# Items of an expert layer: nested branches, the first items' loads, and the order of gathers and stores, all reworked at once

## The chip, the cores and the metric

The kernel runs on one core of a Trainium2 chip. The metric is device time in microseconds of one execution, the median of the runs shown; lower is better. Engines are called TensorE (PE in rows, PEld its weight loads), VectorE (DVE), ScalarE (ACT), GpSimd (POOL) and SyncE (SP, which issues most DMAs).

## What is computed

Three layers follow one another, in float32.

```python
# 1: attention in chunks of 64 positions; 8 batches, 8 heads, 576 positions, head size 64
scores = q_c @ k_c.T / 8; attn = softmax(scores); out = attn @ v_c      # -> x [4608, 512]
# 2: dense layer
h = x @ w_in                       # [4608, 2048]
g = s * relu(h)**2 + b
x = g @ w_out                      # [4608, 512]
# 3: experts; one of 8 for each token, or none
do_compute = x @ w_skip > 0
e_idx = argmax(xc @ w_gate); gate_w = softmax(...)[e_idx]
y[mask] = gate_w * (relu(xc[mask] @ w1[e]) @ w2[e])   # w1 [8,512,1024], w2 [8,1024,512]
out = x; out[do_compute] = xc + y
```

## The kernel before

Every product that must be exact to float32 is made of three: a matrix is split into a high part (a copy by ScalarE into the product format, "split_hi") and a low part (what is left, a subtraction on VectorE, "split_lo"), and low x high, high x low and high x high are added in PSUM.

The 4608 tokens are 36 tiles of 128, in 13 chunks of 2 or 3 tiles (`SIZES`). For each chunk the dense layer runs 16 steps over the 2048 columns: `p1_mm` (a product group of 12), `p1_sq` (ScalarE: relu and square), `p1_g` (scale, bias and split), and two steps later `p2` (a product group into the accumulators). In chunks 0 and 1 the scale and bias are on ScalarE, in the others on VectorE. After a chunk, `evac` stores the plain result to `out`, the logits and the routing (`route_a` to `route_ids`) choose an expert for each token, the rows with their gate value are stored to a table in memory (`x1s`, by `route_row`, 528 values a row), and the token numbers are scattered into lists by expert (`idl`).

All this, and the first two expert items, is ordered by a planner (`Plan.run`): operations have an engine, a cost, what they must follow, and an urgency; the planner simulates the engines and writes instructions in the order that it finds. Each engine then runs its instructions strictly in this order. The planner's names used here: `a12_f`, `q12_f`, `g12_f`, `b12_f` are the four parts of step f of the last chunk (chunk 12), `rw` the stores of x1s rows, `s_n`, `s_1`, `s_2` the count of tokens by expert after eleven chunks and the choice of the two largest experts from it, `s_i`, `s_g` the loads of their lists and the gathers of their tokens, and `s_w00`, `s_w01`, `s_w10`, `s_w11` the loads of the raw weights of these two items (first digit the item, second 0 for `w1`, 1 for `w2`, 2 MB each). The raw weights go where the dense layer's second matrix was: item 0's into the buffers of `w_out` 0 to 7, which `b12_7` reads last, item 1's into 8 to 15, which `b12_15` reads last.

An expert item is one expert and up to 256 of its tokens (full item) or up to 128 (half item). Item 0 and item 1 are the two speculative ones. What is left is counted after the last chunk (`t_n` to `t_c`), and lists of full and half items are made (`tu`, `tb`); their number is only known on the chip, so the code holds 24 full items and 8 half items (twice, for an odd or even number of full items), each behind a branch on the counts `ca` and `ch`. In this data there are 11 full and 4 half items. All engines take each branch for themselves.

A full item (`full_item`) does eight groups `mm1` (12 products each, 256 columns), each followed by a relu and a split of the result, then transposes of the next item's tokens (`x_all`), then eight groups `mm2` (6 products each, 512 columns) into two accumulators. Beside them the next item's weights are split in 16 parts (`split`, u = 0 to 15). At the end `put_add` multiplies by the gate and adds the input row on VectorE, and `put_out` scatters the result to `out` by an indirect DMA on GpSimd. At the start of an item the tokens and weights of the item after next are loaded (`load_x`: a list by SyncE, then two gathers by GpSimd; `load_w`: two loads by SyncE). A half item (`half_item`) is built alike with other shapes: 24 products, 12 transposes, 24 products; four of its 16 splits have their low part on GpSimd (`split_part`). Half items nest: behind a branch that another follows, the item that loads more, in the Else the last one (`final`).

## Time and profile before

| | us |
|---|---|
| median of 3 runs | 1332.43 (1331.69 to 1333.62) |
| the profiled execution, its own time | 1333.88 |
| its span, first to last instruction | 1332.0 |
| TensorE busy | 1289.6 (97%) |
| TensorE weight loads busy | 1152.3 (87%) |
| VectorE busy | 959.4 (72%) |
| ScalarE busy | 582.8 (44%) |
| GpSimd busy | 165.7 (12%) |

Times in rows are us from the start of the span. Busy time is an average over the stages: attention and the dense layer run to about 935, the two speculative items to about 998, the full items to 1256, the half items to the end. The profile names for each instruction what ended the idle time before it. "issue" there means that the engine waited for nothing that the profile shows. TensorE's granted clock is 1.00 at 2.4 GHz and 0.50 at 1.2 GHz; a stretch's value is the mean.

### The profile page before, as it was taken

The page shows a single profiled execution, that of the slowest core. Times are in us where ns is not written, and L with a number is a line of the kernel's source. Part 1 is how long each engine was busy: PE and PEld are TensorE (multiplying, and loading weights), DVE is VectorE, ACT ScalarE, POOL GpSimd, SP SyncE. Part 2 cuts the span into 40 slices and gives each one's busy share as a digit, 9 for nine tenths or more (in the row PEclk, how much of TensorE's full clock was granted, in tenths as well). Part 3 has the DMA queues.
Part 4 walks back from the last instruction along what each step waited for, and adds up shares of the span by engine and source line. Part 5 has one row for each costly group of instructions (what it writes and reads, how often), then busy time and mean ns, then how long its engine had stood idle before and what let it go on. Part 6 is the DMA issues. An engine that isn't in the chain of part 4 may idle for free. (4 is left out here: it accounts for less than half of the span.)

```text
span 1332.0 us, 23920 instructions
## 1 busy us (share of the span) xinstructions
PE 1289.6 (97%) x9112; PEld 1152.3 (87%) x9115; DVE 959.4 (72%) x2341; ACT 582.8 (44%) x1206; POOL 165.7 (12%) x186
## 2 busy tenths in 40 slices
PE   7999999999999999999999999999899999999895
PEld 5888898999998999999999999999788999998773
DVE  6995587659495766859485766757688878787684
ACT  7887533232232333233232333232546656555472
POOL 0000001000101010100101010101122121121252
PEclk9999999999999999999999999999799999999998
DMA  7562324111214142131314131112969565666472
GB/s 270 186 198 104 66 79 88 40 48 48 49 48 73 48 44 77 33 64 49 49 48 73 48 50 56 17 33 81 260 220 391 190 232 221 221 255 220 162 288 90
DMA packets 43019, 160.46 MB, mean 120 GB/s; under 512 B 11370, under 2 KB 11754, under 8 KB 38142
## 3 DMA queue, kind: packets, MB, share of 16 engines
q1 hardware_dynamic: 36526, 142.55, 35.6%
q0 software_dynamic: 6352, 16.12, 3.5%
q8 instruction: 78, 1.28, 0.4%
q14 instruction: 63, 0.52, 0.1%
HBM read 132.68 MB, written 27.20 MB: 120 GB/s over the span
## 5 line engine op out<-in xcount | busy, mean ns | idle before, releaser
L332 ACT ACTIVATE r<-ph 128x384 f32<-128x384 f32 (+1 forms) x208 | 97.0, 466 | 418.0 <-PE ph L325 405.9
L325 PE MATMUL ph<-xh,win_l 128*128 128x384 f32 (+1 forms) x832 | 273.1, 328 | 0.0
L325 PE MATMUL ph<-xh,win_h 128*128 128x384 f32 (+1 forms) x832 | 270.1, 325 | 0.0
L325 PE MATMUL ph<-xl,win_h 128*128 128x384 f32 (+1 forms) x832 | 269.1, 323 | 0.0
L368 PE MATMUL acc<-wout_h,gl 128*128 128x512 f32 x544 | 218.7, 402 | 2.6 <-DVE gl L352 2.4
L349 DVE TENSOR_SCALAR r<-r,sb_sb 128x384 f32<-128x384 f32 (+1 forms) x176 | 84.3, 479 | 180.3 <-ACT r L333 180.0
L368 PE MATMUL acc<-wout_l,gh 128*128 128x512 f32 x544 | 214.1, 394 | 0.0
L368 PE MATMUL acc<-wout_h,gh 128*128 128x512 f32 x544 | 212.6, 391 | 0.0
L388 DVE CUSTOM_DVE_ANT_0 junk<-x,wl_sb 128x512 bf16<-128x512 f32 x270 | 185.7, 688 | 5.7
L325 PEld LDWEIGHTS ph<-xh,win_l 128*128 128x128 f32 x832 | 156.6, 188 | 7.0
L325 PEld LDWEIGHTS ph<-xl,win_h 128*128 128x128 f32 x832 | 156.7, 188 | 6.3
L325 PEld LDWEIGHTS ph<-xh,win_h 128*128 128x128 f32 x832 | 156.5, 188 | 0.0
L714 PE MATMUL ac<-win_h,hhl 128*128 128x512 f32 x480 | 155.1, 396 | 1.1 <-DVE hhl L795 1.0
L352 DVE TENSOR_TENSOR gl<-r,gh 128x384 fp32r<-128x384 f32 (+1 forms) x208 | 109.7, 527 | 31.4 <-ACT gh L339 25.1
L696 PE MATMUL ph<-xh,win_l 128*128 128x256 f32 x416 | 119.5, 287 | 5.7 <-ACT r L702 4.5
L368 PEld LDWEIGHTS acc<-wout_h,gh 128*128 128x128 f32 x544 | 102.1, 188 | 23.1
L368 PEld LDWEIGHTS acc<-wout_h,gl 128*128 128x128 f32 x544 | 102.1, 188 | 21.8 <-DVE gl L352 4.5
L696 PE MATMUL ph<-xl,win_h 128*128 128x256 f32 x416 | 119.0, 286 | 0.4 <-DVE xl L674 0.4
L658 DVE TENSOR_TENSOR win_l<-wlr,win_h 128x512 fp32r<-128x512 f32 x130 | 89.9, 712 | 40.9 <-ACT win_h L655 40.8
L696 PE MATMUL ph<-xh,win_h 128*128 128x256 f32 x416 | 118.9, 286 | 0.0
L368 PEld LDWEIGHTS acc<-wout_l,gh 128*128 128x128 f32 x544 | 102.4, 188 | 13.5
L714 PEld LDWEIGHTS ac<-win_h,hhl 128*128 128x128 f32 x480 | 90.9, 189 | 21.0 <-DVE hhl L795 2.6
(232 smaller groups left out, 2046.2 us busy)
## 6 DMA issues: line engine op xcount, KB each, us to landing
whr<-in_w SPq DMA_DIRECT2D x18, 2048.0 KB, 8.6
wlr<-in_w SPq DMA_DIRECT2D x18, 2048.0 KB, 11.4
qk<-in_qk SPq DMA_DIRECT2D x32, 512.0 KB, 4.1
x1s<-x SPq DMA_DIRECT2D x36, 264.0 KB, 9.3
out<-x SPq DMA_DIRECT2D x36, 256.0 KB, 2.3
v<-in_v SPq DMA_DIRECT2D x32, 256.0 KB, 2.9
stg<-in_w_in SPq DMA_DIRECT2D x16, 512.0 KB, 4.3
stg<-in_w_out SPq DMA_DIRECT2D x16, 512.0 KB, 4.2
```

The lines of the kernel that those rows point to most:

```text
L325: T.matmul(ph, a[:, f, k * P:(k + 1) * P], b[c][:, k, :n], start=(i == 0), stop=(i == 11))
L332: S.activation(out=r, in_=ph_t.pop((c, f)), func=AF.Relu)
L349: V.tensor_scalar(out=r, in0=r, scalar1=sb_sb[:, 0:1], scalar2=sb_sb[:, 1:2], op0=ALU.mult, op1=ALU.add)
L352: V.tensor_tensor(out=gl, in0=r, in1=b32(gh), op=ALU.subtract)
L368: T.matmul(acc[c][j], a[:, j * P:(j + 1) * P], wo(b, f), start=(f == 0 and n == 0), stop=(f == NF - 1 and n == 2))
L388: V.tensor_tensor_reduce(out=junk, in0=x1t[T0[c] + j][:, :D], in1=wl_sb[0][:, i, :], op0=ALU.mult, op1=ALU.add, scale=1.0, scalar=0.0, acc ...
L658: ENG[eng].tensor_tensor(out=win_l[:, u, :], in0=raw[u // 8][:, u % 8, :], in1=b32(win_h)[:, u, :], op=ALU.subtract)
L696: T.matmul(ph, w[:, f, j * P:(j + 1) * P], r2[x][:, j, :], start=(n == 0), stop=(n == 11))
L714: T.matmul(ac[t], r2[h][:, f, t * P:(t + 1) * P], w[:, 8 + f, :], start=(f == 0 and n == 0), stop=(f == 7 and n == 2))
```

## The change

1. The last chunk's scale and bias go to ScalarE (`ON_ACT`).
2. `s_n`, `s_1`, `s_2` get an earlier, higher urgency. The x1s stores of chunks 11 and 12 come behind the weight loads of items 0 and 1 in the order, and `s_w01` is planned after `b12_10` instead of `b12_7`.
3. Full items: `put_add`, `put_out` and the last two splits of item k-1 are done inside item k, after its first product group (`full_add`, `full_out`); after the last full item they stand alone (`full_end`). The tokens are loaded one item ahead instead of two, into two buffers instead of three, and the gathers come between the adds and the stores. The list for the stores is loaded a second time, into its own buffer (`pidx`).
4. Branches: the code that runs when there is another full item falls through; in each item a hint is placed that tells each engine by the count which way the next branch will go, after `mm2` group 3 in a full item, at the start in a half item.
5. Half items: `chain` (items that load another, with a hint), then `pair` (the last two, which load nothing, without a branch between them). The result of item j-1 is put after item j's first product group. All splits have their low part on VectorE.

```diff
--- before.py
+++ after.py
@@ -31,6 +31,7 @@
 PADB = E * CAP
 IDN = PADB + 256
 XW = 528
+ON_ACT = (0, 1, 12)
 NFULL = 24
 NHALF = 8
 SCALE = 0.125
@@ -332,7 +333,7 @@
         S.activation(out=r, in_=ph_t.pop((c, f)), func=AF.Relu)
         S.activation(out=r, in_=r, func=AF.Square)
         r_t[c, f] = r
-        if c < 2:
+        if c in ON_ACT:
 
             gh = gp.tile([P, CH], F32R, tag="gh", name="gh")[:, :n]
             S.activation(out=r, in_=r, func=AF.Identity, scale=sb_sb[:, 0:1], bias=sb_sb[:, 1:2])
@@ -342,7 +343,7 @@
     def p1_g(c, f):
         n = SIZES[c] * P
         r = r_t.pop((c, f))
-        if c < 2:
+        if c in ON_ACT:
             gh = gq.pop((c, f))
         else:
             gh = gp.tile([P, CH], F32R, tag="gh", name="gh")[:, :n]
@@ -736,9 +737,41 @@
             put_add(ac, xg, t)
             put_out(idx, t)
 
-    def full_item(xg, idx, raw, xn):
-
-        for f in range(8):
+    ALL = [getattr(mybir.EngineType, n) for n in ("PE", "DVE", "Activation", "Pool", "SP")]
+
+    def full_add(k):
+
+        fo[:] = []
+        for t in range(2):
+            put_add(r2["ac"], r2["xg", k % 2], t)
+            fo.append(ot[t])
+        for u in (14, 15):
+            split(r2["raw"][(k + 1) % 2], u)
+
+    def full_out(k):
+        for t in range(2):
+            ot[t] = fo[t]
+            put_out(r2["pidx", k % 2], t)
+
+    fo = []
+
+    def full_end(k):
+        full_add(k)
+        full_out(k)
+
+    def full_item(k, hint):
+
+        raw, xn = r2["raw"][(k + 1) % 2], r2["xg", (k + 1) % 2]
+        load_idx(ld(r2["tu"], k, 1, PADB), r2["pidx", k % 2], 2)
+        mm1(0)
+        if k:
+            full_add(k - 1)
+            load_x(ld(r2["tu"], k + 1, 1, PADB), r2["idx", (k + 1) % 2], xn, 2)
+            full_out(k - 1)
+        load_w(ld(r2["tu"], k + 2, 0, E - 1), r2["raw"][k % 2])
+        mm1_relu(0)
+        mm1_h(0)
+        for f in range(1, 8):
             mm1(f)
             mm1_relu(f)
             mm1_h(f)
@@ -748,24 +781,17 @@
         for f in range(8):
             mm2(f, r2["ac"])
             split(raw, f + 6)
-        split(raw, 14)
-        put_add(r2["ac"], xg, 0)
-        split(raw, 15)
-        put_add(r2["ac"], xg, 1)
-        put_out(idx, 0)
-        put_out(idx, 1)
+            if f == 3:
+                hint()
 
     def load_w(e, raw):
         load_w1(e, raw[0])
         load_w2(e, raw[1])
 
-    def half_item(j, odd, final):
-        xg, idx = r2["xgb", j % 3], r2["idxb", j % 4]
+    def half_item(j, odd, load, last, hint=None):
+
         raw, mine = r2["raw"][(j + 1 + odd) % 2], r2["raw"][(j + odd) % 2]
         late = range(12, 16)
-
-        def split_part(raw, u):
-            split(raw, u, "POOL" if u in (1, 4, 9, 13) else "DVE")
 
         def load_next():
             b = ld(r2["tb"], j + 2, 1, PADB)
@@ -794,32 +820,41 @@
             S.activation(out=hh, in_=tp, func=AF.Copy)
             V.tensor_tensor(out=hl, in0=tp, in1=b32(r2["hh"])[:, 4 * i:4 * i + 4, 0:P], op=ALU.subtract)
 
+        if hint:
+            hint()
         m1(0, (0, 1, 2, 3))
+        if j:
+            half_end(j - 1)
         relu(0)
         if j:
             for u in late[:2]:
-                split_part(mine, u)
+                split(mine, u)
         m1(1, (0, 1))
         htr(0)
         if j:
-            split_part(mine, late[2])
+            split(mine, late[2])
         m1(1, (2, 3))
         relu(1)
         if j:
-            split_part(mine, late[3])
-        if not final:
+            split(mine, late[3])
+        if load:
             load_next()
+        if not last:
             x_all(r2["xgb", (j + 1) % 3], [r2["tpx"]])
         mm2(0, r2["ac"][:1])
         htr(1)
         for f in range(1, 8):
             mm2(f, r2["ac"][:1])
-            if not final:
-                split_part(raw, f - 1)
-        if not final:
+            if not last:
+                split(raw, f - 1)
+        if last:
+            half_end(j)
+        else:
             for u in range(7, late[0]):
-                split_part(raw, u)
-        put(r2["ac"][:1], xg, idx)
+                split(raw, u)
+
+    def half_end(j):
+        put(r2["ac"][:1], r2["xgb", j % 3], r2["idxb", j % 4])
 
 
     with tc.manual_schedule():
@@ -984,15 +1019,15 @@
             end = f == NF - 1
             add(f"a{k}", "PE", 1.95 * n, lambda c=c, f=f: p1_mm(c, f), ([f"cl{2 * f}"] if c < 2 else []) + w, i, ["ph"],
                 [("xhl", f"hi{T0[c]}")] if end else [])
-            add(f"q{k}", "ACT", (.55 + 1.29 * n) if c < 2 else (.28 + .66 * n), lambda c=c, f=f: p1_sq(c, f), [f"a{k}"], i + HURRY,
-                ["r", "g"] if c < 2 else ["r"], [("ph", f"a{k}")])
-            add(f"g{k}", "DVE", (.07 + .39 * n) if c < 2 else (.8 + .6 * n), lambda c=c, f=f: p1_g(c, f), [f"q{k}"], i + HURRY,
-                [] if c < 2 else ["g"], [("r", f"q{k}")])
+            add(f"q{k}", "ACT", (.55 + 1.29 * n) if c in ON_ACT else (.28 + .66 * n), lambda c=c, f=f: p1_sq(c, f), [f"a{k}"], i + HURRY,
+                ["r", "g"] if c in ON_ACT else ["r"], [("ph", f"a{k}")])
+            add(f"g{k}", "DVE", (.07 + .39 * n) if c in ON_ACT else (.8 + .6 * n), lambda c=c, f=f: p1_g(c, f), [f"q{k}"], i + HURRY,
+                [] if c in ON_ACT else ["g"], [("r", f"q{k}")])
             w = [f"b{c}_{f - 1}"] if f else []
             if c < 2 and not f:
                 w = ["lo3", "lo4"] if c else ["sub3", "cp3"]
             add(f"b{k}", "PE", 1.95 * n, lambda c=c, f=f: p2(c, f), [f"g{k}"] + ([f"cl{2 * f + 1}"] if c < 2 else []) + w,
-                i + LAG - .5, [] if f else banks(c), [("g", f"{'q' if c < 2 else 'g'}{k}")])
+                i + LAG - .5, [] if f else banks(c), [("g", f"{'q' if c in ON_ACT else 'g'}{k}")])
 
 
         for c in range(NCH):
@@ -1069,9 +1104,10 @@
                 r2["es", m] = ld(r2["se"], 0, 2 * m, E - 1)
             (load_w2 if which else load_w1)(r2["es", m], r2["raw"][m][which])
 
-        add("s_n", "PE", .1, spec_count, [f"rb{L - 2}"], i, ["sc"])
-        add("s_1", "DVE", 1.8, spec_first, ["s_n"], i, [], [("sc", "s_n")])
-        add("s_2", "DVE", 2.2, spec_second, ["s_1"], i)
+        h = iL - NF
+        add("s_n", "PE", .1, spec_count, [f"rb{L - 2}"], h, ["sc"])
+        add("s_1", "DVE", 1.8, spec_first, ["s_n"], h + HURRY, [], [("sc", "s_n")])
+        add("s_2", "DVE", 2.2, spec_second, ["s_1"], h + HURRY)
         add("s_i", "DMA", 4.5, spec_rows, ["s_2"] + [f"rs{L - 2}_{j}" for j in range(SIZES[L - 2])], i)
         pl.ops[f"rs{L - 1}_0"][2].append("s_i")
         pl.ops[f"rb{L - 1}"][2].append("s_n")
@@ -1079,9 +1115,12 @@
             add(f"s_g{m}", "POOL", 3.0, lambda m=m: spec_gather(m), ["s_i"] + [f"rw{t}" for t in range(T0[L - 1])], i,
                 ["e", "e"] if m else ["qk"])
             add(f"s_d{m}", "DMA", 1.5, None, [f"s_g{m}"], i)
+        for c, w in ((L - 1, "s_w01"), (L, "s_w11")):
+            for t in range(T0[c], T0[c + 1]):
+                pl.ops[f"rw{t}"][2].append(w)
         for which in range(2):
             add(f"s_w0{which}", "DMA", 5.9 + 2 * (1 - which), lambda w=which: spec_w(0, w),
-                [f"b{L}_7", "s_2", f"s_d{which}"] + (["s_w00"] if which else []), iL + 10)
+                [f"b{L}_{7 + 3 * which}", "s_2", f"s_d{which}"] + (["s_w00"] if which else []), iL + 10)
             add(f"s_w1{which}", "DMA", 5.9 + 2 * (1 - which), lambda w=which: spec_w(1, w),
                 [f"b{L}_{NF - 1}", "s_w01"] + (["s_w10"] if which else []), iE)
 
@@ -1093,7 +1132,7 @@
             hl = bg.tile([P, 2, 8, 256], F32R, tag="big", name="hhl")
             r2["hh"], r2["hl"] = hl[:, 0], hl[:, 1]
             for i in range(4):
-                r2["idx", i] = rp.tile([P, 2], I32, name=f"idx{i}")
+                r2["idx" if i < 2 else "pidx", i % 2] = rp.tile([P, 2], I32, name=f"idx{i}")
                 r2["idxb", i] = rp.tile([P, 1], I32, name=f"idxb{i}")
 
         def mm1_first(m, f):
@@ -1119,7 +1158,6 @@
                 load_idx(ld(r2[nm], m, 1, PADB), r2["idx", m], 2)
             else:
                 if m == 0:
-                    r2["xg", 2] = [op_.tile([P, XW], F32, tag="x1", name=f"xg2{i}") for i in range(2)]
                     r2["xgb", 0] = [op_.tile([P, XW], F32, tag="x1", name="xgb0")]
                     r2["xgb", 1] = [row("v")]
                 load_idx(ld(r2[nm], m, 1, PADB), r2["idxb", m], 1)
@@ -1213,28 +1251,48 @@
         ch = nc.values_load(cnt[0:1, 1:2], min_val=0, max_val=NHALF)
         odd = nc.values_load(cnt[0:1, 2:3], min_val=0, max_val=1)
 
-        def halves(j, odd):
-            if j == NHALF - 1:
-                half_item(j, odd, True)
-                return
-            with tc.If(ch > j + 1, preferred_fallthrough_block=True) as more:
-                half_item(j, odd, False)
-                halves(j + 1, odd)
-            with more.Else():
-                half_item(j, odd, True)
-
-        with ExitStack() as cs:
-            for k in range(NFULL):
-                cs.enter_context(tc.If(ca > k))
-                load_x(ld(r2["tu"], k + 2, 1, PADB), r2["idx", (k + 2) % 4], r2["xg", (k + 2) % 3], 2)
-                load_w(ld(r2["tu"], k + 2, 0, E - 1), r2["raw"][k % 2])
-                full_item(r2["xg", k % 3], r2["idx", k % 4], r2["raw"][(k + 1) % 2], r2["xg", (k + 1) % 3])
+        def fulls(k):
+            with tc.If(ca > k, preferred_fallthrough_block=True, label=f"full{k}"):
+                full_item(k, (lambda: tc.mark_branch_hint_location(f"full{k + 1}", ca > k + 1, engines=ALL))
+                          if k + 1 < NFULL else lambda: None)
+                if k + 1 < NFULL:
+                    fulls(k + 1)
+
+        def chain(j, odd):
+
+            more = j + 3 < NHALF
+            half_item(j, odd, True, False, (lambda: tc.mark_branch_hint_location(f"half{odd}{j}", ch > j + 3, engines=ALL))
+                      if more else None)
+            if more:
+                with tc.If(ch > j + 3, preferred_fallthrough_block=True, label=f"half{odd}{j}") as c:
+                    chain(j + 1, odd)
+                with c.Else():
+                    pair(j + 1, odd)
+            else:
+                pair(j + 1, odd)
+
+        def pair(j, odd):
+            half_item(j, odd, False, False)
+            half_item(j + 1, odd, False, True)
+
+        def halves(odd):
+            with tc.If(ch > 0, preferred_fallthrough_block=True):
+                with tc.If(ch > 2, preferred_fallthrough_block=True) as c:
+                    chain(0, odd)
+                with c.Else():
+                    with tc.If(ch > 1, preferred_fallthrough_block=True) as d:
+                        pair(0, odd)
+                    with d.Else():
+                        half_item(0, odd, False, True)
+
+        fulls(0)
         with tc.If(odd > 0, preferred_fallthrough_block=True) as arm:
-            with tc.If(ch > 0):
-                halves(0, 1)
+            full_end(0)
+            halves(1)
         with arm.Else():
-            with tc.If(ch > 0):
-                halves(0, 0)
+            with tc.If(ca > 0, preferred_fallthrough_block=True):
+                full_end(1)
+            halves(0)
 
 
 def layouts(q, k, v, moe_w_in, moe_w_out, moe_s, moe_b, moe2_w_skip, moe2_w_gate, moe2_w1, moe2_w2):
```

## Rows read from the trace of the kernel before

**Rows 1.** Windows: length; PE, PEld, DVE, ACT, POOL busy; granted clock, DMA share, GB/s.
```profile
890.00:936.00 46.00, 45.92 (x300) 40.83 (x300) 35.28 (x124) 15.37 (x37) 9.11 (x13) 1.00 0.29 76
...
1050.00:1250.00 200.00, 200.00 (x1315) 184.07 (x1314) 162.88 (x314) 114.32 (x228) 40.84 (x35) 1.00 0.61 224
...
1260.00:1270.00 10.00, 9.71 (x42) 7.96 (x43) 1.38 (x2) 2.71 (x5) 0.99 (x2) 0.83 0.96 366
```

**Rows 2.** Timeline of TensorE, 912 to 964: start, length, instruction [idle before, releaser].
```profile
912.29 0.39 PE L368 MATMUL acc<-wout_h,gh 128*128 128x512 f32 x1
...
934.65 0.40 PE L368 MATMUL acc<-wout_h,gh 128*128 128x512 f32 x1
...
936.43 1.95 PE L407 MATMUL pl<-wlt,et 128*128 128x9 f32 x16
...
942.47 0.58 PE L696 MATMUL ph<-xh,win_l 128*128 128x256 f32 x1 [0.45 <-DVE win_l L658]
...
945.84 0.37 PE L696 MATMUL ph<-xh,win_l 128*128 128x256 f32 x1
...
957.27 0.58 PE L696 MATMUL ph<-xh,win_l 128*128 128x256 f32 x1 [2.91 <-ACT r L702]
...
963.26 0.62 PE L714 MATMUL ac<-win_h,hhl 128*128 128x512 f32 x2
```

**Rows 3.** Timelines of GpSimd and ScalarE, 920 to 957.
```profile
921.40 1.05 POOL L647 DMA_INDIRECT xgs<-x1s,idxs  x1 [59.75 <-DMA idxs<-idl]
...
936.97 3.21 ACT L655 ACTIVATE win_h<-whr 128x512 fp32r<-128x512 f32 x6
...
955.80 1.15 ACT L655 ACTIVATE win_h<-wlr 128x512 fp32r<-128x512 f32 x2 [3.84 <-DMA wlr<-in_w]
```

**Rows 4.** Timeline of SyncE's DMA issues, 921 to 937.
```profile
921.72 0.34 SPq L633 DMA_DIRECT2D whr<-in_w  x1
...
931.84 1.63 SPq L458 DMA_DIRECT2D x1s<-x  x3
...
933.68 2.51 SPq L636 DMA_DIRECT2D wlr<-in_w  x1
```

**Rows 5.** Timeline of TensorE, half items.
```profile
1260.29 0.76 PE L782 MATMUL ph<-win_h,xl 128*128 128x512 f32 x1 [3.85 <-DVEq L1226]
...
1263.68 0.39 PE L782 MATMUL ph<-win_h,xh 128*128 128x512 f32 x1
...
1274.19 0.39 PE L782 MATMUL ph<-win_h,xl 128*128 128x512 f32 x1
...
1302.10 0.39 PE L714 MATMUL ac<-win_h,hhl 128*128 128x512 f32 x1
...
1307.64 0.60 PE L782 MATMUL ph<-win_h,xl 128*128 128x512 f32 x1 [5.15 <-issue]
```

**Rows 6.** Timeline of VectorE, splits of half item 1.
```profile
1285.36 6.42 DVE L658 TENSOR_TENSOR win_l<-whr,win_h 128x512 fp32r<-128x512 f32 x6
...
1291.71 1.88 DVE L658 TENSOR_TENSOR win_l<-wlr,win_h 128x512 fp32r<-128x512 f32 x3
```

**Rows 7.** DMA issues: line, engine, count, KB, median us from issue to landing.
```profile
wlr<-in_w SPq DMA_DIRECT2D x18, 2048.0 KB, 11.4
...
xg<-x1s,idx POOLq DMA_INDIRECT x26, 7.2
```

**Rows 8.** Timelines of GpSimd and TensorE in full item 10.
```profile
1234.12 1.29 POOL L727 DMA_INDIRECT out<-et,idx  x1 [17.70 <-DVE et L724]
...
1238.61 1.11 POOL L647 DMA_INDIRECT xg<-x1s,idx  x1 [0.30 <-issue]
...
1244.49 0.60 PE L667 MATMUL tp2a<-idt,xg 128*128 128x128 f32 x4
```

**Rows 9.** The chain that ended last: start, us, what.
```profile
1322.52 0.04 POOLq L1220
...
1322.61 0.04 POOLq L1220
```

## The prediction

> **What bounds the kernel now.** I read the busy time by stretches first. In the steady part TensorE sets the pace: it is busy for all 200 us of 1050 to 1250, where the eleven full items run, at the upper clock level [rows 1]. Nothing off TensorE can shorten that part, and the dense part ahead of 890 looks the same. So I looked for stretches where TensorE is idle or slow, and there are two: the change from the dense layer to the experts (935 to 963), and the half items at the end (from 1256).
>
> At the first place the list of TensorE's instructions shows the last product of the dense layer ending at 935.04, then transposes and logits (1.95 us of them from 936.43), and the first product of expert item 0 only at 942.47. There is a second hole of 2.91 us before 957.27. After both, products go at the lower level, 1.2 GHz: until 945.84 and until 963.26 they are spaced nearly twice as wide as later [rows 2]. ScalarE shows why: the first splits of item 0's first weights run at 936.97, although the item needs them to start, and its splits of the second weights begin at 955.80 after 3.84 us of waiting for that load; the relus that free TensorE's buffers are queued behind them [rows 3]. SyncE's list shows why the loads are late: the first went out at 921.72, the second at 933.68, behind three stores of x1s rows that left at 931.84 [rows 4]. The first waited for nothing but the choice of expert: its buffer was last read by dense step 7, whose last product starts at 912.29 (eight steps of six products follow it) [rows 2].
>
> At the second place TensorE stands still for 3.85 us ahead of half item 0 and for 5.15 us ahead of half item 3, the last [rows 5]. Nothing it computes with is late there: the first is put down to the branch at L1226 (leaving the nest of full items after the eleventh), the second to "issue". Both are jumps over code that isn't run: 13 unused full items, and the nest of half items up to its Else. At the restart the products are slow again, to 1263.68; the granted clock of 1260 to 1270 is 0.83, which is 3.4 us at 1.2 GHz [rows 1, 5]. Half items 1 and 2 take 28.30 us together (1274.19 to 1302.49), where item 0, with 1.7 us lost to the clock, took 13.90: 12.2 us of TensorE work each, and 1.95 us each of something else [rows 5]. That is VectorE: six splits that run while GpSimd splits too take 6.42 us, three without it 1.88 us [rows 6].
>
> **The change, part by part.**
>
> *Early choice of the two first experts, loads ahead of the x1s stores.* The same 22 small VectorE instructions, moved forward. GpSimd had stood 59.75 us waiting for the indices that come out of them [rows 3], so the data is there long before. Then the first load is bound by its buffer and goes out near 913, the second right behind it or some steps later. Even at the 11.4 us median landing of the second kind [rows 7] the first lands near 924, and the second, started by about 920, near 932, both ahead of 935. The splits (3.21 us for six, 0.53 each [rows 3]) then run beside the last dense steps. What is left between 935.04 and item 0 is the work of the logits, about 3.0 us (two transposes of 0.44, 1.95, 0.2), and I take 1.0 us of waiting: 7.43 - 4.0 = 3.4 us gained. The clock then has no hole to fall in: half of 942.47 to 945.84 is 1.7. The wait of 2.91 goes, as the second weights are there, and with it half of 957.27 to 963.26, 3.0. Together **11.0 us**. Bounds: 0, if the splits stay behind other ScalarE work, and 13, if the logits too are hidden.
>
> *Last chunk's scale and bias on ScalarE.* Sixteen steps, two more activations each; half as wide as a split, so at most 32 x 0.53 = 17 us on ScalarE, which is busy 15.37 of 46 us there [rows 1, 3]. With 16 splits (8.5) it is 41 of 46: it fits, narrowly, and VectorE (35.28 busy) is relieved for its half of the splits. On the path: 0. If it didn't fit, the item would start late by the overflow; a few us, inside the bounds just given.
>
> *x1s stores after the loads.* What is late next are gathers of all rows, the tables' items. They follow item 0's end, which itself moves forward by the same amount as the tables; 0.
>
> *Full items.* The stores of item k-1 move behind item k's first product group and behind the next gathers; one small load of indices more per item. TensorE is at 200 of 200 us here, so no gain is possible; cost 0 while the gather is in time. GpSimd stored at 1234.12 and gathered until the second gather at 1238.61; TensorE's transposes of what was gathered an item earlier come at 1244.49 [rows 8]. Now the rows for the very next transposes are gathered, in the place of the stores: second issue near 1235.7, landing 7.2 us later [rows 7], 1242.9, so 1.6 us in time. In the new order VectorE's two adds must be done before (the buffer is reused); they were the condition for the store at 1234.12 as well.
>
> *Hints and falling through.* If the target of a jump is fetched while the item before it runs, a branch costs what an already fetched one does: the three exits of L1220 pass at 0.09 us each [rows 9]. There are four or so at the first place. I leave 1.0 us at both, between 0.2 and the whole hole. 3.85 becomes 1.0, gain 2.85; 5.15 becomes 1.0, gain 4.15; the slow starts go, half of 3.39 for the first, 1.7, and the same for the second. Together **10.4 us**.
>
> *All half splits on VectorE.* 16 x 0.63 (1.88 for three [rows 6]) is 10.1, with four more instructions of the same size about 12.5 us per item, against 12.2 of TensorE. So 12.5 in place of 14.15, for two items: **3.3 us**. Bounds 0 (VectorE stays the limit) and 3.9. The last loads, for items that don't exist, are dropped; nobody waits for them: 0.
>
> Sum: 11.0 + 10.4 + 3.3 = 24.7 us. The profiled execution took 1333.88, so 1309.2. It lay 1.45 above the median shown, so **1308** as the median. A difference under 0.2% (2.7 us) can't be told from none.
>
> **Rivals.**
>
> *The hints do nothing.* The two jumps stay, one now after half item 1. For it: no row of this trace shows a hinted jump, and both jumps are far. Against it: fetched branches at 0.09 us are there, and a hint gives the fetch half an item or more. Then 10.4 us are lost: 1318. A rule speaks for this: the Trainium skill, "Runtime: NRT & Kernel Launch", Instruction fetch mechanics, says that instruction fetch runs ahead strictly in sequence, and a taken branch outside the resident pages waits for a load of its page. The two holes agree with its second half; by the first half a hint has nothing to act on and the time is this rival's.
>
> *The start of the experts doesn't move.* ScalarE at 41 of 46 us is in order: if it stands before a load, the dense products wait instead, and the hole moves into chunk 12. Then 11.0 are lost: 1319. Against it: both loads have 3 to 11 us of slack by medians.
>
> *Slower: the gathers of full items are late.* They are now needed in the item that issues them. Margin 1.6 us over a landing of 7.2; from 8.8 us each item waits. If they land like the weights that start beside them, 11.4 us, that is 2.6 us, and a hole of that size also costs slow products (2.91 cost 3.0 above): 5.6 for ten items, 56 against 24.7 gained: 1364. Without the slow clock it turns at 2.5 us per item, a landing of 11.3. For it: weight loads take most of the traffic here. Against: the gathers go first now, where stores went ahead of them.
>
> *Slower: hints pull in the wrong page.* If fetching the target drops the page that comes next, each of ten full items stops as half item 0 did, 3.85 us and 1.7: 55 more, 1363.
>
> **How the numbers follow.** Everything as worked out, 0.65. Hints do nothing, 0.14; start doesn't move, 0.12; gathers late, 0.05; wrong pages, 0.03; gains and losses that cancel, 0.01. The first three are faster, 0.91; slower 0.08; same 0.01. The range reaches from 1301 (no time left at the branches, 2.0; logits hidden, 2; splits better, 0.6, and some us elsewhere in 963 to 1010) to 1320, past the two rivals at 1318 and 1319; what it leaves out is about 0.12.
>
> **What would show it.** The first weight load near 913, ahead of any x1s store of chunk 11; the first item product at 936 to 938, no wait for the second weights, a granted clock of 1.00 through 930 to 970. Full items at the same period of TensorE, transposes not waiting. Before the first half item and before item 2 a hole near 1 us or none, clock 1.00; half items 12.5 us apart, VectorE splits at 0.63. It is wrong if the holes stay, if ScalarE waits for a load while dense products run, or if transposes in full items wait for GpSimd's gathers.

## The result and the profile after

The changed kernel takes 1319.07 us (median of 4 runs, 1317.26 to 1319.32), the kernel before on the same chip 1332.29: a ratio of 0.9896 (95% interval 0.9879 to 0.9914), so 13.2 us were gained. From profiled execution to profiled execution it is 16.6 us (1333.88 to 1317.26), with spans of 1332.0 and 1315.3.

I cut both spans at the same places of TensorE's timeline:

| stretch | before, us | after, us | difference |
|---|---|---|---|
| start to the end of the last dense product | 935.05 | 942.71 | +7.66 |
| from there to item 0's first product | 7.42 | -0.16 | -7.58 |
| item 0 | 31.65 | 27.28 | -4.37 |
| item 1 | 24.12 | 24.14 | +0.02 |
| eleven full items | 258.20 | 258.27 | +0.07 |
| stop ahead of the first half item | 3.85 | 1.33 | -2.52 |
| four half items | 61.40 | 51.74 | -9.66 |
| end of the last product to the end | 10.31 | 9.99 | -0.32 |

They add up to -16.70, the difference of the spans. The first goes against the forecast and takes 7.66 back; item 1 and the full items were forecast at 0, and the rest go the way of the forecast.

Windows of the changed kernel (columns as in [rows 1], which they answer):

```profile
913.00:915.00 2.00, 2.00 (x16) 1.91 (x15) 0.42 (x1) 1.07 (x3) 0.21 (x5) 1.00 2.20 82
915.00:917.00 2.00, 2.00 (x14) 1.79 (x14) 0.27 (x1) 1.60 (x4) 0.00 (x0) 1.00 0.97 49
917.00:919.00 2.00, 2.00 (x13) 1.74 (x12) 0.15 (x1) 1.33 (x3) 0.00 (x0) 1.00 0.00 0
...
923.00:925.00 2.00, 2.00 (x13) 1.74 (x13) 0.00 (x0) 0.00 (x0) 0.00 (x0) 1.00 0.96 401
...
930.00:940.00 10.00, 8.69 (x38) 7.82 (x39) 4.46 (x8) 8.07 (x18) 0.00 (x0) 0.66 0.39 158
...
1050.00:1250.00 200.00, 199.07 (x1282) 181.38 (x1281) 156.21 (x306) 113.08 (x223) 33.12 (x32) 1.00 0.62 215
1253.00:1263.00 10.00, 9.43 (x47) 7.85 (x48) 4.99 (x8) 5.07 (x10) 3.11 (x3) 1.00 0.88 344
```

The full items are as dense as before, and the half items start at the upper clock. But 930 to 940 has a granted clock of 0.66, inside the dense layer, where the kernel before had 1.00. TensorE's timeline there (beside [rows 2]):

```profile
931.32 0.80 PE L369 MATMUL acc<-wout_h,gl 128*128 128x512 f32 x1 [5.27 <-DVE gl L353]
...
934.04 0.41 PE L326 MATMUL ph<-xh,win_l 128*128 128x256 f32 x1
...
937.20 0.28 PE L326 MATMUL ph<-xh,win_l 128*128 128x256 f32 x1
...
942.32 0.39 PE L369 MATMUL acc<-wout_h,gh 128*128 128x512 f32 x1
942.55 0.28 PE L697 MATMUL ph<-xh,win_l 128*128 128x256 f32 x1
...
969.83 0.38 PE L697 MATMUL ph<-xh,win_l 128*128 128x256 f32 x1 [0.82 <-ACT xh L671]
```

Dense products stand still for 5.27 us, then take 0.41 instead of 0.28 us until 937.20. Behind that, item 0 follows the last dense product without a gap. What they stand for is two engines back: TensorE waits for VectorE's low part, VectorE for ScalarE's `p1_sq`, and ScalarE stands in the splits of the first weights. SyncE's issues, GpSimd's scatters of chunk 11's token numbers, and ScalarE, three timelines (beside [rows 3, 4]):

```profile
913.34 0.35 SPq L634 DMA_DIRECT2D whr<-in_w  x1
913.90 0.35 SPq L637 DMA_DIRECT2D wlr<-in_w  x1
914.71 1.43 SPq L459 DMA_DIRECT2D x1s<-x  x3
```

```profile
909.31 1.02 POOL L487 DMA_INDIRECT idl<-ids_sb,si  x1 [31.46 <-DVE oacc L482]
...
911.94 0.97 POOL L487 DMA_INDIRECT idl<-ids_sb,si  x1 [0.30 <-issue]
```

```profile
928.37 0.63 ACT L656 ACTIVATE win_h<-whr 128x512 fp32r<-128x512 f32 x1 [6.02 <-DMA whr<-in_w]
```

The load goes out at 913.34, as forecast, but ScalarE can read it only at 928.37, 15.0 us later. From the windows above, little moves for most of that time: 401 GB/s only from 923 on. The windows count a packet's bytes where the packet starts, so the 0 GB/s of 917 to 919 says that no packet starts there, not that none is on its way (the DMA share of 2.20 in 913 to 915 belongs to packets that last beyond those 2 us). Three scatters of 128 numbers of 4 bytes went out just ahead of it. DMA issues of 905 to 935 in the changed kernel:

```profile
idl<-ids_sb,si POOLq DMA_INDIRECT x3, 8.1
```

They take 8.1 us to land; the last, issued from 911.94, is through near 920.

The trace's records of single DMA packets show where the time goes. The load is 128 packets of 16 KB. The scatters' 96 packets are recorded as over by 913.7, 0.01 us each. The load's first 16 packets start between 914.3 and 916.8 and take up to 8.4 us; those from 925 on take 0.6.

The other end. TensorE at the half items (beside [rows 5]), and VectorE there (beside [rows 6]):

```profile
1253.57 0.47 PE L808 MATMUL ph<-win_h,xl 128*128 128x512 f32 x1 [1.33 <-DVEq L1255]
...
1265.99 0.39 PE L808 MATMUL ph<-win_h,xl 128*128 128x512 f32 x1
...
1278.47 0.39 PE L808 MATMUL ph<-win_h,xl 128*128 128x512 f32 x1
...
1286.57 0.50 PE L715 MATMUL ac<-win_h,hhl 128*128 128x512 f32 x1 [1.58 <-DVE hhl L821]
...
1292.60 0.39 PE L808 MATMUL ph<-win_h,xl 128*128 128x512 f32 x1
```

```profile
1250.22 0.69 DVE L659 TENSOR_TENSOR win_l<-wlr,win_h 128x512 fp32r<-128x512 f32 x1 [0.67 <-ACT win_h L656]
1253.75 1.41 DVE L725 SCALAR_TENSOR_TENSOR et<-ac,xg 128x512 f32<-128x512 f32 x2 [2.83 <-DVEq L1255]
...
1267.43 2.50 DVE L659 TENSOR_TENSOR win_l<-wlr,win_h 128x512 fp32r<-128x512 f32 x4
...
1283.96 0.75 DVE L725 SCALAR_TENSOR_TENSOR et<-ac,v 128x512 f32<-128x512 f32 x1 [1.48 <-PE tp2a L818]
```

Splits take 0.62 us (2.50 for four). Half items 0 and 1 take 12.42 and 12.48 us. The far jump (a branch over code that isn't run) ahead of item 2 (1278.47) costs TensorE nothing, but VectorE stands 1.48 us there. The row names a TensorE transpose, which was over at 1283.16 already; VectorE's own branch starts at 1280.83, and the first instruction behind it at 1283.86 (splits queued ahead of the branch run in between). TensorE waits for VectorE at 1286.57, and the item takes 14.13 us.

### The profile page after: what moved, and what is told of

The parts are those of the page before. It is cut to its first block, busy times and chain, and to the rows that moved or that the text cites. A ratio compares the mean times of both kernels' runs of the same rounds, so it can differ in the third digit from the quotient of the medians.

```text
span 1315.3 us, 24016 instructions
## 1 busy us (share of the span) xinstructions
PE 1284.0 (98%) x9112; PEld 1148.7 (87%) x9115; DVE 939.3 (71%) x2321; ACT 598.5 (46%) x1238; POOL 140.8 (11%) x171
## 4 chain that ended last, share of the span: by engine, by line
PE 73%; DMA 12%; issue 7%; DVE 3%; ACT 3%; POOL 1%; SPq 0%; another core or an unknown queue 0%; POOLq 0%; ACTq 0%; DVEq 0%
PE ph L326 28%; PE acc L369 27%; PE ac L715 5%; PE ph L697 4%; DMA out<-et,idx 4%; DMA xg<-x1s,idx 4%; PE po L298 2%; PE sc L231 2%; DMA whr<-in_w 1%; PE tp L283 1%; DMA idx<-idl 1%; DMA qk<-in_qk 1%; ACT e L259 1%; DVE stg L193 1%; DMA stg<-in_w_out 1%
## 5 line engine op out<-in xcount | busy, mean ns | idle before, releaser
L350 DVE TENSOR_SCALAR r<-r,sb_sb 128x384 f32<-128x384 f32 (+1 forms) x160 | 77.7, 486 | 170.3 <-ACT r L334 170.0
L656 ACT ACTIVATE win_h<-wlr 128x512 fp32r<-128x512 f32 x136 | 83.4, 630 | 59.1 <-PE ac L715 53.9
```

The source lines that it names most:

```text
L350: V.tensor_scalar(out=r, in0=r, scalar1=sb_sb[:, 0:1], scalar2=sb_sb[:, 1:2], op0=ALU.mult, op1=ALU.add)
L656: S.activation(out=win_h[:, u, :], in_=raw[u // 8][:, u % 8, :], func=AF.Copy)
```

## The experiments

All are edits of the changed kernel, each beside runs of the kernel before on its chip. "Dense" is the time from the issue of the first weights' load to the end of the last dense product, so that what came earlier doesn't enter; "half" is from the first product of the half items to the end of the last; "tail" what follows. These three are of the profiled execution.

| kernel | us (runs) | ratio to before, interval | dense | half | tail |
|---|---|---|---|---|---|
| changed | 1319.07 (4) | 0.9896 (0.9879 to 0.9914) | 29.4 | 51.7 | 10.0 |
| no_scatter11 | 1315.29 (1) | 0.9845 | 22.0 | 52.6 | 9.5 |
| x1s_later | 1318.31 (1) | 0.9868 | 29.7 | 51.6 | 10.1 |
| late_splits | 1316.82 (4) | 0.9866 (0.9839 to 0.9893) | 22.5 | 51.5 | 10.0 |
| scatter_after_load | 1315.56 (4) | 0.9857 (0.9839 to 0.9875) | 22.0 | 51.5 | 10.1 |
| no_hints | 1324.30 (4) | 0.9885 (0.9856 to 0.9913) | 31.7 | 56.4 | 7.6 |
| pool_splits | 1332.22 (10) | 0.9945 (0.9929 to 0.9962) | 30.3 | 60.5 | 10.1 |
| stores_first | 1327.54 (1) | 0.9916 | 30.6 | 51.5 | 7.6 |
| act_01 | 1319.44 (1) | 0.9856 | 23.7 | 51.5 | 10.0 |
| after_again | 1321.71 (6) | 0.9898 (0.9864 to 0.9931) | 30.1 | 51.5 | 10.1 |
| scatter_after_load_again | 1313.62 (6) | 0.9838 (0.9807 to 0.9870) | 22.0 | 51.8 | 10.1 |
| no_hints_again | 1322.74 (6) | 0.9903 (0.9871 to 0.9935) | 30.8 | 56.5 | 7.6 |
| pool_no_hints | 1326.39 (10) | 0.9941 (0.9920 to 0.9962) | 30.6 | 58.9 | 10.0 |

The kernel before took 1335.97 us beside the four rows that follow the changed kernel, 1338.76 beside the next four and 1336.27 beside the last four (medians), so ratios and stretches are compared, not times. The expectations name times of the first chip: there a ratio is to be multiplied by 1332.29. Six runs of the changed kernel on one chip reach from 1318.21 to 1326.12 us, so the ratio of a single run, which has no interval, says little; its stretches are read instead.

### What delays the first weights

The theory: chunk 11's scatters, just ahead of the load, hold it up, and ScalarE, standing in the split that needs it, stops the dense products. The rivals: the x1s stores and the second load beside it do; or ScalarE's added work in the last chunk ends the dense part late by itself.

**no_scatter11** leaves out one part of the work, as its expectation says:

```diff
         t = T0[c] + j
+        if c == NCH - 2:
+            return
```

> This kernel leaves out the scatter of chunk 11's token numbers into the lists, so those tokens miss the experts; all other work is as in the changed kernel. Theory S (the first weight load is held for some 8 us by the three scatters of 4-byte items issued just before it, 909.3 to 912.9): the load, which took 15.0 us from 913.34, lands within 9 us, before 923; ScalarE's wait of 6.0 us and TensorE's hole of 5.27 us in chunk 12 are gone, the clock stays at 1.00, and the time is 1309 to 1312, some 8 us under the 1319 of the changed kernel. Rival X (the x1s stores issued 0.8 us behind the loads hold them) and rival W (the two loads share the bandwidth, each taking twice its time): the load still lands near 928 and the time stays near 1317 to 1319.

Measured: ScalarE waits for no load, dense products don't stop, and the dense stretch falls from 29.4 to 22.0 us. The ratio makes 1311.7 us of the first chip, as forecast. The second load still goes out right behind the first here, so sharing with it isn't the cause.

**x1s_later** moves the stores that follow the loads further back:

```diff
-        for c, w in ((L - 1, "s_w01"), (L, "s_w11")):
+        for c, w in ((L - 1, "s_w11"), (L, "s_w11")):
```

> The three x1s stores of chunk 11 come behind all four weight loads of items 0 and 1 in SyncE's order, some 30 us later; nothing else is changed. Theory S: no change of the landing, 928 within 1 us, time 1317 to 1320. Rival X: the load lands by 923, the hole of 5.27 us is gone, 1309 to 1312. Rival W: no change.

Measured: no change of the landing. ScalarE waits 7.33 us for the load, the dense stretch is 29.7 us. The stores of x1s rows beside the load are not the cause. (The time came out lower than expected, 0.9868; it is a single run, and the full items are 1.2 us shorter in it.)

**late_splits** tells the planner that the load takes longer, so that ScalarE's splits come later in the order:

```diff
-            add(f"s_w0{which}", "DMA", 5.9 + 2 * (1 - which), lambda w=which: spec_w(0, w),
+            add(f"s_w0{which}", "DMA", 5.9 + 10 * (1 - which), lambda w=which: spec_w(0, w),
```

> The planner is told that the first weight load takes 15.9 us instead of 7.9, so that it puts the first split of these weights later in ScalarE's order; the load itself is issued at the same time. If the hole in chunk 12 comes only from ScalarE standing in order before a load (whatever holds the load), it goes: 5.3 us and the slow products after it, 8 us in all; up to 2 us come back at the start of item 0, where fewer splits are ready: 1311 to 1314. Rival: ScalarE is simply too full in chunk 12 (41 of 46 us by the forecast's own count), and the work it did not do there is missing at the start of item 0: 1317 or more.

Measured: the scatters still go out ahead of the load, but ScalarE now comes to its first split at 934.27, 17.4 us after the load's issue, and doesn't wait; 1.07 us of TensorE's stop are left (dense 22.5 us). In time the gain is not clear of the spread: the interval overlaps the changed kernel's. The stretch shows that it is ScalarE's place in the order, ahead of `p1_sq`, that makes a late load stop the dense products.

**scatter_after_load** keeps all work and turns the two transfers round: GpSimd reads one number of the first weights ahead of chunk 11's scatters.

```diff
+        if c == NCH - 2 and j == 0:
+            G.tensor_copy(rp.tile([1, 1], F32, name="here"), r2["raw"][0][0][0:1, 7, 511:512])
...
-        pl.ops[f"rs{L - 1}_0"][2].append("s_i")
+        pl.ops[f"rs{L - 1}_0"][2].extend(["s_i", "s_w00"])
+        for j in range(1, SIZES[L - 1]):
+            pl.ops[f"rs{L - 1}_{j}"][2].append(f"rs{L - 1}_{j - 1}")
```

> GpSimd reads one element of the first weights before it issues the scatters of chunk 11, so that these go out when the load has landed. Theory S: the load lands in 6 to 9 us, by 922; no hole in chunk 12; the second weights are then held by the scatters and land near 934, still ahead of their use after 942; 1309 to 1312. Rivals X and W: the load lands near 928 as before, the scatters come later still, and the time stays at 1317 to 1320.

Measured: dense 22.0 us, no stop; the second weights weren't held either, ScalarE waits for neither load. The ratio makes 1313.2 us of the first chip, a little above what was expected: item 1 takes 2.3 us more than in the changed kernel and the full items 0.9, so of 7.4 us some 4 are left in the span. That the edit costs this is not shown: in after_again, the changed kernel once more, item 1 takes 26.50 us (24.14 here above) and the full items 258.54. The second time, beside the changed kernel on one chip:

> The changed kernel with the scatters of chunk 11's token numbers held back until the first weights have landed, again, now beside the changed kernel on one chip. If the scatters are what delays the load: 4 us faster than the changed kernel (7 us at the end of the dense part, some 3 given back in item 1 and the full items). If the earlier gain was the chip's: the same time.

> The changed kernel itself, beside the next three on one chip: 0.989 to 0.990 of the time before. If the stop of ScalarE before the first weights' load is not chance, it is there again (5 to 7 us).

Measured: 1313.62 against 1321.71 us, and no run of the one (1312.82 to 1315.67) is as slow as the fastest of the other (1318.21 to 1326.12): 8.1 us, twice the 4 that were expected, since nothing was given back. In the changed kernel the stop was there again, 6.28 us on TensorE. GpSimd's timeline and a window of scatter_after_load_again, whose first load goes out at 917.92:

```profile
925.81 0.18 POOL L488 COPY here<-whr 1x1 f32<-1x1 f32 x1 [43.38 <-DMA whr<-in_w]
926.66 1.05 POOL L489 DMA_INDIRECT idl<-ids_sb,si  x1 [0.67 <-issue]
```

```profile
921.00:926.00 5.00, 5.00 (x34) 4.53 (x33) 0.85 (x2) 3.02 (x8) 0.18 (x1) 1.00 1.01 429
```

The load is there after 7.9 us instead of 15.0 (429 GB/s are both loads together). The packet records agree over all runs: in the nine profiles whose first load goes out right behind the scatters, the slowest of its first 16 packets takes 8.4 to 9.7 us; in the four in which the scatters are left out or come later, 1.4 to 1.7. Why three small scatters do this is not shown: no run tells their item size from their way through GpSimd's queue.

**act_01** leaves the last chunk's scale and bias on VectorE:

```diff
-ON_ACT = (0, 1, 12)
+ON_ACT = (0, 1)
```

> Scale and bias of the last chunk stay on VectorE; all else is the changed kernel. If ScalarE's added work in chunk 12 (about 17 us of it) is what makes the dense part end late, the dense part ends some 6 us earlier and the time is 1312. If it is the late landing of the first weights with ScalarE standing before it, ScalarE stands as long (5 to 7 us), the hole in the dense products stays, and the time is 1317 to 1322.

Measured: dense 23.7 us, nearly the first forecast, but not for the reason given there: the edit also changed the planner's order, and the scatters now come at 924.25, behind the load of 917.89. ScalarE and GpSimd of act_01, two timelines:

```profile
925.60 1.15 ACT L656 ACTIVATE win_h<-whr 128x512 fp32r<-128x512 f32 x2 [0.73 <-DMA whr<-in_w]
...
936.74 1.15 ACT L656 ACTIVATE win_h<-wlr 128x512 fp32r<-128x512 f32 x2 [3.02 <-DMA wlr<-in_w]
```

```profile
924.25 1.02 POOL L487 DMA_INDIRECT idl<-ids_sb,si  x1 [40.91 <-DVE oacc L482]
```

The first weights, ahead of the scatters, took 7.7 us; the second, which the scatters ran into, 18.3 (issue at 918.47), and a stop of 2.06 us on TensorE follows that wait. So it fits the scatters once more, though here the order of other work changed with them. scatter_after_load has ScalarE's added work and ends its dense part even sooner, 22.0 us, so that work costs nothing once the load is in time.

### Gathers and stores

**stores_first** puts `full_out(k - 1)` ahead of `load_x`:

```diff
             full_add(k - 1)
+            full_out(k - 1)
             load_x(ld(r2["tu"], k + 1, 1, PADB), r2["idx", (k + 1) % 2], xn, 2)
-            full_out(k - 1)
```

> In full items the two stores go out before the gathers of the next item's rows instead of after them, both still behind the first product group. By the prediction's margin (gathers 1.6 us in time) two stores of 1.3 us ahead of them make the transposes wait 1.0 us per item; by the trace of the changed kernel, where two transposes wait 0.36 and 0.47 us for a gather and the margin is about nothing, 2 to 2.6 us in nearly each of ten full items, 20 us or more with what the clock loses. Rival: GpSimd stands elsewhere and the order of its four DMAs is free; then full items stay at 24.1 us.

Measured: the eleven full items take 261.86 us, 3.6 more than in the changed kernel. Transposes wait for gathers in five items, 0.22 to 0.88 us, 2.73 in all. Both sizes were too large. Whether the order costs anything is not shown: with the stores behind the gathers, the full items of the other kernels take 257.07 to 261.21 us, and transposes wait for gathers in none to four items, up to 1.69 us once and 3.36 in all. Landings scatter about the time at which the rows are needed. The changed kernel shows it; GpSimd's and TensorE's timelines in its full item 10 (beside [rows 8]):

```profile
1228.61 0.98 POOL L648 DMA_INDIRECT xg<-x1s,idx  x1 [18.24 <-DVE et L725]
1229.89 1.16 POOL L648 DMA_INDIRECT xg<-x1s,idx  x1 [0.30 <-DVE win_l L659]
```

```profile
1240.65 0.66 PE L668 MATMUL tp2b<-idt,xg 128*128 128x128 f32 x4 [0.47 <-DMA xg<-x1s,idx]
```

The rows are needed 10.3 us after the second issue (1240.18), not 8.8 as forecast, and this landing took 10.8, not 7.2.

### Hints and half items

**no_hints** takes both kinds of hints out:

```diff
-                full_item(k, (lambda: tc.mark_branch_hint_location(f"full{k + 1}", ca > k + 1, engines=ALL))
-                          if k + 1 < NFULL else lambda: None)
+                full_item(k, lambda: None)
...
-            half_item(j, odd, True, False, (lambda: tc.mark_branch_hint_location(f"half{odd}{j}", ch > j + 3, engines=ALL))
-                      if more else None)
+            half_item(j, odd, True, False, None)
```

> The changed kernel without its branch hints, in full and in half items; all else stays. Theory H (the hints start the fetch of the code behind a far jump): the stop ahead of the first half item goes back from 1.33 to some 3.9 us, a stop of about 5 us appears ahead of half item 2 (now the jump into the last pair), and each is followed by some 1.7 us lost to products at 1.2 GHz; half items end 8 to 10 us later, 1327 to 1329 us, full items keep their 24.1 us. Rival P (code is fetched strictly in sequence, a hint has nothing to act on, and the shorter stops come from the new shape of the branches): no stop changes, 1319 us within 2.

> The changed kernel without hints, now beside the changed kernel on one chip. From the profile of the run before, where the stop ahead of half item 2 was 3.3 us and the half items took 56.4 us instead of 51.7: 4 to 5 us slower than the changed kernel. If hints cost as much elsewhere as they give there: the same.

TensorE and VectorE of no_hints_again, two timelines:

```profile
1260.84 0.47 PE L808 MATMUL ph<-win_h,xl 128*128 128x512 f32 x1 [1.04 <-DVEq L1255]
...
1289.31 0.77 PE L808 MATMUL ph<-win_h,xl 128*128 128x512 f32 x1 [3.43 <-issue]
```

```profile
1257.79 0.69 DVE L659 TENSOR_TENSOR win_l<-wlr,win_h 128x512 fp32r<-128x512 f32 x1 [0.67 <-ACT win_h L656]
1261.27 1.41 DVE L725 SCALAR_TENSOR_TENSOR et<-ac,xg 128x512 f32<-128x512 f32 x2 [2.79 <-DVEq L1255]
...
1291.16 0.75 DVE L725 SCALAR_TENSOR_TENSOR et<-ac,v 128x512 f32<-128x512 f32 x1 [1.45 <-issue]
```

Measured, three things. The stop ahead of the first half item does not come back without hints (1.04 us): they didn't shorten it. What is left of it, 1.0 to 1.4 us in most profiles, is mostly TensorE's own four branches there and the hint's instructions. The stop ahead of half item 2 does come back, 3.43 us (3.29 in the first run), with products at the lower clock behind it (0.63 instead of 0.39 us), and the half items take 56.4 to 56.5 instead of 51.5 to 51.7 us. VectorE's own stop there is the same with and without hints, 1.45 and 1.48 us. And the time hardly follows (0.9885 makes 1317 us of the first chip, rival P's time): 1322.74 against 1321.71 us, and the runs of the two overlap, so that a gain in time by the hints is not shown. In the two profiles, of the 4.9 us 2.5 come back in the tail (7.6 instead of 10.1) and 0.7 at the first half item. The short tail is not the hints' doing: stores_first has hints and a tail of 7.6 too, pool_no_hints below has none and 10.0. The difference lies in one place: from GpSimd's last branch to its closing instruction pass 0.36 or 0.37 us in the three profiles with 7.6, and 2.6 to 2.9 in the others (tails of 9.5 to 10.3). What makes that branch cheap in three kernels stays open.

**pool_splits** gives splits 1, 4, 9 and 13 of the half items back to GpSimd, and **pool_no_hints** takes the hints out of that kernel as well:

```diff
+        def split_part(raw, u):
+            split(raw, u, "POOL" if u in (1, 4, 9, 13) else "DVE")
...
-                split(raw, f - 1)
+                split_part(raw, f - 1)
```

> In the half items the low parts of splits 1, 4, 9 and 13 go back to GpSimd, as in the kernel before; the rest is the changed kernel. Theory V (VectorE is slowed while GpSimd splits beside it, and sets the pace of half items): VectorE's splits cost 1.0 us and more each while GpSimd works, half items 0 and 1 take 14.1 us instead of 12.4, the end is 3 to 5 us later, near 1323. Rival: moving the sums behind the first product group is what shortened the half items; then 12.4 us stays and the time is 1319.

> Half items' splits on GpSimd as before, and no hints. With hints this kernel stopped for 5.1 us ahead of half item 2, as the kernel before did, which has none. If the hint did nothing there, the stop stays at 5.1 us and the time at that of the kernel with hints; if it hid a part, the stop grows to some 8 us. The half items without the stop stay near 14.4 us if it is VectorE, slowed by GpSimd, that sets their pace.

TensorE and VectorE of pool_no_hints, two timelines:

```profile
1287.82 0.47 PE L811 MATMUL ph<-win_h,xl 128*128 128x512 f32 x1 [4.26 <-issue]
```

```profile
1280.42 6.39 DVE L659 TENSOR_TENSOR win_l<-whr,win_h 128x512 fp32r<-128x512 f32 x6
1286.73 1.89 DVE L659 TENSOR_TENSOR win_l<-wlr,win_h 128x512 fp32r<-128x512 f32 x3
```

Beside GpSimd a split takes VectorE 1.07 us (6.39 for six), alone 0.63. In pool_splits half item 1 takes 19.47 us, of which 5.11 are a stop; the other 14.36 are near the 14.15 of the kernel before. Item 0, which carries no debt yet, takes 12.35, so 14.1 for both, as expected, was half wrong. Without hints on either side the splits on GpSimd cost 2.5 us of the half items (58.9 against 56.4; in time 1326.39 against 1322.74 us on the same chip). With hints they cost 8.8 us (60.5 against 51.7), because the stop ahead of item 2 was there in spite of the hint, 5.11 us, against 4.26 without one. The same hint in the same place acts in one kernel and not in the other. Why is not settled.

## Why the prediction was right in its range and 11 us off

From profiled execution to profiled execution 24.7 us were forecast and 16.6 came: 8.1 of the 11 us are terms of the sum, 6.7 of them the first. The other 3 are runs: the forecast took 1.45 us off because the profiled run before lay above its median, and the profiled run after lies 1.81 below its own; the rest is rounding. The range held by luck as much as by reckoning. "Everything as worked out", at 0.65, did not happen; 1319.07 lies 0.9 us inside an upper end that was drawn to take in the rivals at 1318 and 1319, and two terms that came near, the hints and the full items, did so partly by other means than those worked out.

- **Early choice and loads ahead of the stores, 11.0 us: got 4.3** (+7.66 - 7.58 - 4.37). Every step behind the load came as said: load at 913.34, no wait for the second weights in item 0, the gap ahead of item 0 gone, logits hidden too. The step that failed is "even at the 11.4 us median landing", with the 3 to 11 us of slack that follow from it. It landed after 15.0. And the slack was counted to 935, where the item starts, but ScalarE comes to the first split at 922.35 (6.02 us ahead of 928.37), 9.0 us after the issue: a landing after 11.4 would have made it wait 2.4 us as well. The 5.27 us stop with the slow products behind it is the 7.4 us by which the dense stretch exceeds the 22.0 of the four profiles whose load is not held up or not waited for (22.0 to 22.5). I had named it as what would prove me wrong: ScalarE waiting for a load while dense products run. It is the second rival's mechanism ("the hole moves into chunk 12"), and its time, 1319, though not all of the 11.0 was lost. The rows before held the warning. The second load went out at 933.68 and ScalarE read it at 955.80 [rows 3, 4], 22 us, twice the median, and right behind scatters of the same kind, which I hadn't looked for. The last of them (the kernel before, GpSimd's timeline):

```profile
930.72 0.97 POOL L486 DMA_INDIRECT idl<-ids_sb,si  x1 [0.30 <-issue]
```

- **Scale and bias on ScalarE, 0:** right in cost (scatter_after_load). ScalarE is busy for 29.72 of the last 46 us of the dense layer, not 41, and stands for 6.02; it was not too full, but its order passed the wait on to the dense products.
- **x1s stores behind the loads, 0:** right as far as shown; moving chunk 11's further back changed neither the landing nor the dense stretch (x1s_later).
- **Full items, 0:** +0.07 us, a sum of two opposite things. In the kernel before, the first full item takes 25.12 us (TensorE waits 1.57 us for ScalarE at 1004.28), most others 23.29; after the change it takes 23.29, and four later ones lose 2.1 us together. The margin of 1.6 us was no margin: two gathers came 0.36 and 0.47 us late.
- **Hints, 10.4 us:** the sizes were near, half of the mechanism wrong. The first stop, 3.85 us, was not TensorE's jump: TensorE has passed its four branches by 1257.2 and waits for VectorE to leave the nest. VectorE's last add in the kernel before ended 2.05 us after TensorE's last product. The row of the kernel before (VectorE's timeline):

```profile
1257.74 0.75 DVE L724 SCALAR_TENSOR_TENSOR et<-ac,xg 128x512 f32<-128x512 f32 x1
```

  What takes VectorE's time there is its own jump. A view of the branch's line lists the branches and semaphores themselves (count, length in ns, first and last start); before, then after:

```profile
L1226 DVEq COMPARE_BRANCH  x2: 47/57/67, 1257.3 to 1260.2; - x2
L1226 DVEq EVENT_SEMAPHORE  x1: 21/21/21, 1260.1 to 1260.1; - x1
```

```profile
L1255 DVEq COMPARE_BRANCH  x2: 61/72/84, 1250.2 to 1253.2; - x2
L1255 DVEq EVENT_SEMAPHORE  x1: 21/21/21, 1253.1 to 1253.1; - x1
```

  From VectorE's branch to the first instruction behind it pass 2.86 us before, 2.90 after and 2.88 to 2.91 in the three profiles without hints: neither the hint nor the change made this jump shorter. But before, it began 0.83 us after TensorE's last product; since the adds moved behind it, it begins 2.0 us ahead of that product's end (VectorE's last work ahead of the exit ends at 1250.91, TensorE's at 1252.24) and is hidden. no_hints has the short stop without a hint. The row said so: "DVEq" [rows 5]. The second stop was TensorE's own jump: it went with the hint and is back without it. The 2.85 + 1.7 us of the first place belong to the moved adds (read from the traces; no run moves the adds alone), which the sum had not counted on: that this half came out near is luck. Of the 4.15 + 1.7 of the second, the hints brought 4.7 to 4.9 in the half items; in time, 1.0 us that is not clear of the spread.
- **All half splits on VectorE, 3.3 us: 2.5**, by the two kernels without hints, no_hints and pool_no_hints. Stops and half items together gave 12.2 us (2.52 + 9.66) of the 13.7 forecast; VectorE's own stop of 1.48 us is most of what is missing.
- **The rival that hints do nothing** is true of the first stop, false of the second. The rule behind it, of the Trainium skill, "Runtime: NRT & Kernel Launch", Instruction fetch mechanics (fetch runs ahead strictly in sequence, and a taken branch outside the resident pages waits for its page), agrees with no_hints, with pool_splits and with VectorE's 2.9 us. The changed kernel, where TensorE passes the same jump without a stop, speaks against its first half.
- **The slower rivals** didn't come: in the changed kernel gathers are late by under 0.5 us in two items (by up to 1.69 us in the other kernels), and no full item stops at a branch.

## What to carry to other kernels

A load's landing is read at its place, in the order in which transfers went out, not from the median of all loads of its kind: a few hundred scattered words ahead of it can double it. An engine that stands early in its order for a load passes the wait to everything queued behind it; put either the load ahead of small scatters or the wait behind the work that others need. And a stop at a branch can be another engine's jump: look which engine leaves the branch last, and move its closing work behind the branch, so that its jump begins earlier and runs beside what the others still do.

The version that beats both kernels is scatter_after_load: 0.9838 of the time before, where the changed kernel has 0.9898 on the same chip.

## What was unexpected of the hardware

- Three scatters of 128 numbers of 4 bytes (1.5 KB in all) held up 2 MB loads issued after them by 7 us and more: 15.0 us to land behind them, 7.9 ahead of them, 18.3 with them in between. It is the first packets behind the scatters that take up to 8.4 us instead of under 2. The Trainium skill, "DMA: Bandwidth & Descriptors", Why small descriptors are slow (HBM only), puts the price of small transfers at a few cycles a packet and 32 bytes of metadata each; no such price explains 7 us for 384 numbers, and the measurement decides.
- VectorE's jump out of the nest of full items takes 2.86 to 3.15 us in 13 of 14 profiles, with and without hints. In late_splits alone it takes 0.7, and TensorE's stop there is 1.32 us as in the others, so VectorE no longer sets it.
- A branch hint removed TensorE's stop of 3.3 to 3.4 us in every profile of the kernels with all splits on VectorE, and did not in the one with four on GpSimd (5.11 us with it, 4.26 without). VectorE's jump at the same place it left as it was.
